# The first three loads of a kernel's middle stage, moved by one step and behind another load

## The chip, the cores and the metric

The kernel runs on one core of a Trainium2 chip. A core has a matrix engine (TensorE, PE in the profile; its weight loads are listed apart as PEld), a vector engine (VectorE, DVE), an activation engine (ScalarE, ACT), a general engine (GpSimd, POOL) and a queue engine (SyncE, SP) that here does nothing but issue transfers between memory and the core's on-chip buffers. Each engine works through its own list of instructions in order. Products are accumulated in PSUM banks of 128 x 512 words. The metric is the time of one execution in microseconds; smaller is better.

## The reference

The input `x` has 2048 rows of 576 numbers. Two kinds of layer alternate, each applied to the normalized rows and added to `x`:

```python
x = x + A(layernorm(x), seq_re, seq_im, hid_re, hid_im)
x = x + B(layernorm(x), k, v, shift_k, ssm_k, ssm_D)
x = x + A(layernorm(x), seq_re, seq_im, hid_re, hid_im)
x = x + B(layernorm(x), k, v, shift_k, ssm_k, ssm_D)
```

`A` is the real part of a two-dimensional Fourier transform, written with matrices: `a = x @ hid_re.T`, `b = x @ hid_im.T`, and `y = seq_re @ a - seq_im @ b`. `B` does not need the layer's data until its last step: it forms `kv` from `k`, `v` and a short convolution over four rows, convolves it along the 2048 rows with `ssm_k` (in the reference by an FFT of length 4096), adds `kv * ssm_D`, and multiplies the result into its normalized input. So the long convolution is the same in both `B` layers, and can be computed once, beside the first `A` layer.

## The kernel before

Every product is made in a two-part form: a float32 number is split into a rounded high part (ScalarE, a copy) and a low remainder (VectorE, a subtraction), and three products high-high, high-low and low-high are summed. `split` does it (lines 99 and 100).

**The first layer.** `layer` swaps the order of the two transforms: first along the sequence, then along the hidden axis. It goes through 128 steps, `n` = 0 to 127: four blocks `tb` of 512 output columns, in each the real and the imaginary part (`g`), in each 16 blocks `k` of 128 rows. A step multiplies one row block by one 128 x 512 tile of `c_mat`: twelve products into four banks (named `s`) and two into a fifth (`rm`). `load_c` loads the tile of a step two steps ahead, into a raw buffer of the ring `craw`, and splits it into one of three tiles `cs`. After steps 31, 63 and so on a block is complete; `hidden` multiplies it by the 576 x 576 hidden-axis matrix `W`, in eight half tiles of 27 products each (`bk<-w,u` in the profile), chunk 8 of the reduction last. `added` holds the last addition of such a half tile to the residual (line 289). The eight half tiles of block 0 wait in `pending` and must be done ahead of the last step of block 1's real part, step 47, so that W has to be there then.

**W.** `load_w` is a generator. From step `W_FROM` = 41 on it is called twice a step, in the middle and at the end, until all nine chunks are under way: chunk 8 first, then 0 to 7, so that chunk 6 comes at the end of step 44 and chunk 7 in the middle of step 45. A chunk is 128 x 576 numbers, loaded by SP into one of three buffers `wl` taken in turn, and split into the tile `w`. For the imaginary part (chunks 4 to 7) the sign is turned in the split (ScalarE line 242, VectorE line 243).

**The convolution.** `branch` is a generator that computes `B`'s convolution in three stages beside the first layer: a first Fourier stage (products `bf`, results stored by ScalarE's queue to the tensor `td`), a middle stage of 64 parts that reads `td`, and a last stage. Its F1 stage ends at step 42. The next call of it sets up the middle stage: it lays new rings over buffers of the first stage, cuts the ring `craw` from three raw tiles to two, loads the small matrices `midc` on POOL's queue, and gives out the first three loads from `td` with `load_feed`. These go on SP (line 169), into two tiles in `flts` (ring `land`) and one in the tile `mid`. From step `MID_FROM` = 47 on the middle stage is paced by a cost account: `passed` counts what the layer has done, `spent` what the branch has, and `next(br)` is called while the branch is behind. A part splits its loaded tile (`act_split`: ScalarE line 514, VectorE line 520), multiplies it (three products into each of two banks, `bk<-mid`), forms a complex product (lines 532 to 535), splits, transforms back and stores.

**What sets the order.** The order in which each engine meets its instructions is planned when the kernel is built, by a scheduler that follows the written order where nothing else binds it and the readiness of buffers and data in its own estimate of time. `tc.issue_after(i)` binds it: every instruction written inside that block which goes to `i`'s engine is placed behind `i` on that engine. It adds no wait between engines. `behind(...)` does this for several instructions, and `load_after` puts a load behind the latest load of `c_mat` (`anchor[-1]`).

**Around the change.** In the loop over the first layer, at line 808, stands the call that sets up the middle stage:

```python
        if whole is not None and not part and n >= W_FROM and len(W) < 9:
            with behind(*stored):
                next(wl)
        if whole and n == MID_LOAD:
            next(br)
```

`whole` is true at the end of a step. The functions that the diff touches:

Of the kernel before, what the change touches and what calls it, by code (L numbers as in the profile page):

```python
# [15 lines left out]
P = 128  # L16
# [19 lines left out]
W_FROM = 41  # L36
HOLD = 125
W_SAVE = 60
MID_LOAD = 44
MID_FROM = 47  # L40
I2_END = 111
PREP = 113
# [24 lines left out]
def fnet_h3_kernel(ctx: ExitStack, tc: tile.TileContext, x, c_mat, w_re, w_im, k_pad, v, shift_k,  # L67
                   ssm_k, ssm_d, f1c, i2c, midc, out):
    nc = tc.nc
# [28 lines left out]
    def split(h, l, src):  # L98
        a = nc.scalar.activation(h, src, AF.Copy).ins  # L99
        return a, nc.vector.tensor_tensor(l, src, h.bitcast(F32), OP.subtract).ins  # L100

    @contextmanager
    def behind(*instructions):
        with ExitStack() as stack:
            for i in instructions:
                stack.enter_context(tc.issue_after(i))
            yield
# [8 lines left out]
    def region_a(dt, name):  # L116
        return sb.tile([P, 9 * 2 * D], dt, tag="ra", name=name)

    def region_b(dt, name):
        return sb.tile([P, 6 * WIDE], dt, tag="rb", name=name)  # L120
# [11 lines left out]
    def lay(t, at, *sizes):  # L132

        for name, words, n in sizes:
            ring.setdefault(name, Ring()).tiles.extend(t[:, at + i * words:at + (i + 1) * words] for i in range(n))
            at += n * words
        assert at <= t.shape[1], (at, t.shape, sizes)
        return at

    def fresh(*names):  # L140
        for name in names:
            ring[name] = Ring()

    def two(v):
        return v.rearrange("p (a n) -> p a n", a=2)
# [16 lines left out]

    anchor, made, rounded, pows, biased, halved, added, evac, parted, stored = [], [], [], [], [], [], [], [], [], []

    scaled = []

    def load_after(dst, src):
        with tc.issue_after(anchor[-1]):
            return nc.sync.dma_start(dst, src).ins
# [57 lines left out]
    def load_w():  # L227
        lay(flts, SC_AT + CRAW * NT + 4 * D, ("wl", D, 3))
        wg = region_a(FR, "w").rearrange("p (k n) -> p k n", k=9)
        for ch in (8, *range(8)):  # L230
            w = two(wg[:, ch])
            raw = ring["wl"]()
            if ch < 8:
                nc.sync.dma_start(raw, (w_re if ch < 4 else w_im)[(ch % 4) * P:(ch % 4 + 1) * P, :])
            else:
                nc.sync.dma_start(raw[:REM], w_re[NC * P:, :])
                nc.sync.dma_start(raw[REM:], w_im[NC * P:, :])
            for lo, hi, sg in ((0, P, 1 if ch < 4 else -1),) if ch < 8 else ((0, REM, 1), (REM, P, -1)):
                if sg > 0:
                    split(w[lo:hi, 0, :], w[lo:hi, 1, :], raw[lo:hi])  # L240
                else:
                    nc.scalar.activation(w[lo:hi, 0, :], raw[lo:hi], AF.Copy, scale=-1.0)
                    nc.vector.scalar_tensor_tensor(w[lo:hi, 1, :], raw[lo:hi], -1.0,  # L243
                                                   w[lo:hi, 0, :].bitcast(F32), op0=OP.mult,
                                                   op1=OP.subtract)
            W[ch] = w
            yield
        for ch in range(9):
            load_after(w_d[ch], wg[:, ch].bitcast(F32))
            yield  # L250
# [42 lines left out]
    def finish(pending, pieces):  # L293
        while pending and pieces:
            if not isinstance(pending[0], types.GeneratorType):
                pending[0] = hidden(*pending[0])
            if next(pending[0], 0) == 0:
                pending.pop(0)
            else:
                pieces -= 1  # L300
# [433 lines left out]
    def advance(j=None):  # L734
        while to_store:
            load_after(*to_store.pop(0))
        with behind(*halved, *added, *evac):
            for row in list(making):
                if next(row, 0) == 0:
                    making.remove(row)  # L740
            if j is not None:
                making.append(make_x1(j))
                next(making[-1])
# [22 lines left out]
    lay(flts, SC_AT, ("craw", NT, CRAW))  # L766
    br = branch()
    wl = load_w()
    load_x(0)
    warm()  # L770
# [21 lines left out]
    for n, whole in layer(get_x0, lambda j: x[:, j, :], done0, pending):  # L792
        part = whole == "part"
        if part:
            whole = False
        if (whole or whole is not None and n % J < J - 1) and n <= F1_END and not part:
            at = n if whole else n - 0.5
            at16 = 4 + 2 * F1_16
            want = int(4 + F1_16 * at / 8 if at <= 16 else at16 + (68 - at16) * (at - 16) / (F1_END - 16))
            with behind(made[min(n + 2, J - 1)], *evac):  # L800
                while used < want:
                    next(br)
                    used += 1
        if whole is not None and not part and n >= W_FROM and len(W) < 9:
            with behind(*stored):
                next(wl)
        if whole and n == MID_LOAD:
            next(br)
        if n >= MID_FROM:
            if whole is not None:  # L810
                share = (5 if whole else 3) if n % J < J - 1 else (8 if whole else 6)
                passed += STEP * share / 14 * BORDER.get(n % J, 1.05)
            if whole is None or whole and n % 2 == 1 and n % (2 * J) < J - 1 and pending:
                finish(pending, 1)
                passed += PIECE
            while spent < work * min(1.0, passed / total):
                with behind(*added, *evac):
                    spent += next(br, work)
        if not whole:
            continue  # L820
        if n >= W_SAVE and n % 2 == 0:
            next(wl, 0)
        m = n - PREP
        if m == 0:
            lay(flts, SC_AT + CRAW * NT + 2 * D, ("xa", D, 2), ("yb", D, 2))
            old = ring["craw"]
            held = [old(), old()]
            fresh("craw")
            lay(flts, SC_AT + CRAW * NT + 6 * D, ("craw", NT, 1))
            ring["craw"].tiles.extend(held)  # L830
            gate = region_b(F32, "gate")
            lay(gate, 0, ("xa", D, 4), ("yb", D, 4), ("xj", D, 2))
        if 0 <= m and n < HOLD:
            advance(m // 2 if m % 2 == 0 and m < 2 * EARLY else None)
# [340 lines left out]
```

## Time and profile before

| | |
|---|---|
| median of 3 runs | 1185.11 us (1184.79 to 1185.26) |
| the profiled execution, its own time | 1183.61 us |
| its span (first to last instruction) | 1181.8 us |
| TensorE busy | 1167.8 us, 99% |
| VectorE, ScalarE busy | 868.6 us, 650.8 us |
| granted TensorE clock, mean | 0.999 |

In rows of instructions the columns are: start in microseconds, duration, engine, line of the kernel, operation, what is written and read, shape, the count of instructions merged in the row, and in brackets how long the engine had stood idle before it and what released it. Names such as `s`, `bk`, `mid`, `w` are tiles of the program. `SPq` and `ACTq` are the parts of SP and ScalarE that issue transfers; their rows show the issue, not the transfer itself. The steps of the layer are counted here by the pairs of `rm` products: the pair at 206.85 us is that of step 46.

### The profile page before, as it was taken

The numbers are of one execution on the slowest core, as the hardware profiler recorded it, in microseconds if no ns is written. First come the engines' busy times: TensorE is split into PE (matmuls) and PEld (weight loads), VectorE is DVE, ScalarE is ACT, GpSimd is POOL, SyncE is SP. The second block draws the span as 40 slices with busy tenths as digits, with TensorE's granted clock in tenths as the row PEclk, the third lists the DMA queues.
The fourth block names the chain that finished last, engine by engine and source line by source line (L and its number), as shares of the span: only waits on it lengthen the run. The fifth ranks groups of instructions, "written<-read, shape, count | busy, mean of one in ns | idle before, by whom it ended". The sixth has DMA issues, their size and how long they took to land.

```text
span 1181.8 us, 18082 instructions
## 1 busy us (share of the span) xinstructions
PE 1167.8 (99%) x6198; PEld 989.1 (84%) x6198; DVE 868.6 (73%) x1564; ACT 650.8 (55%) x1280; POOL 75.5 (6%) x115
## 2 busy tenths in 40 slices
PE   8999999999999999999999999999999999999997
PEld 6776667988888888888888898888888888889997
DVE  7899983788877778787756765865776777774764
ACT  8865655577766667766645666534444445550210
POOL 2310000000000000001101111000000000001111
PEclk9999999999999999999999999999999999999999
DMA  9879898546666656648966777762872787894621
GB/s 336 284 232 316 263 300 272 160 152 173 213 214 193 203 168 193 190 140 247 270 192 215 249 240 231 247 253 73 257 249 72 221 284 258 260 338 144 219 93 40
DMA packets 147453, 255.64 MB, mean 216 GB/s; under 512 B 16161, under 2 KB 56353, under 8 KB 147362
## 3 DMA queue, kind: packets, MB, share of 16 engines
q1 hardware_dynamic: 111890, 210.17, 55.6%
q10 hardware_dynamic: 28560, 37.91, 9.2%
q0 software_dynamic: 6912, 6.43, 2.5%
q8 instruction: 48, 0.79, 0.3%
q14 instruction: 43, 0.35, 0.1%
HBM read 187.80 MB, written 66.65 MB: 215 GB/s over the span
## 4 chain that ended last, share of the span: by engine, by line
PE 77%; ACT 2%; DVE 2%; DMA 1%; issue 1%; ACTq 0%; DVEq 0%
PE s L76 43%; PE bk L76 30%; PE rm L76 4%; ACT flts L514 1%; ACT mid L514 1%; DVE mid L520 0%; DMA flts<-td 0%; DMA flts<-in_c_mat 0%; ACT mats L99 0%; DVE flts L534 0%; DVE flts L533 0%; DVE flts L532 0%; DVE flts L535 0%; ACTq L550 0%; ACT u L99 0%
## 5 line engine op out<-in xcount | busy, mean ns | idle before, releaser
L76 PE MATMUL s<-mats 128*128 128x512 f32 x2102 | 545.9, 395 | 4.2 <-ACT mats L197 2.4
L76 PEld LDWEIGHTS s<-mats 128*128 128x128 f32 x2102 | 382.7, 188 | 86.1 <-issue 10.9
L100 DVE TENSOR_TENSOR mats<-flts,mats 128x512 fp32r<-128x512 f32 x206 | 140.6, 686 | 50.3 <-ACT mats L99 48.9
L99 ACT ACTIVATE mats<-flts 128x512 fp32r<-128x512 f32 x206 | 128.2, 627 | 81.8 <-PE bk L76 30.7
L76 PE MATMUL bk<-mid 128*128 128x288 f32 x704 | 126.7, 300 | 2.1 <-DVE flts L289 0.8
L76 PEld LDWEIGHTS bk<-mid 128*128 128x128 f32 x704 | 108.6, 188 | 23.0 <-ACT flts L514 5.9
L514 ACT ACTIVATE flts<-bk 128x288 f32<-128x288 f32 (+1 forms) x192 | 76.5, 405 | 90.4 <-PE bk L76 71.6
L76 PE MATMUL bk<-w,u 128*128 128x288 f32 x864 | 120.6, 295 | 0.4 <-DVE w L243 0.4
L76 PEld LDWEIGHTS bk<-w,u 128*128 128x128 f32 x864 | 117.4, 188 | 3.5 <-ACT flts L514 0.9
L520 DVE TENSOR_TENSOR mid<-flts,mid 128x576 fp32r<-128x576 f32 (+1 forms) x149 | 93.3, 627 | 19.1 <-ACT mid L514 16.4
L76 PE MATMUL rm<-mats 128*128 128x512 f32 x304 | 94.5, 390 | 0.2 <-ACT flts L514 0.2
L514 ACT ACTIVATE mid<-flts 128x576 fp32r<-128x576 f32 (+1 forms) x148 | 80.5, 576 | 10.3 <-DVE flts L535 5.1
L289 DVE TENSOR_TENSOR flts<-flts,bk 128x288 f32<-128x288 f32 x48 | 21.8, 453 | 68.3 <-PE bk L76 65.9
L76 PE MATMUL bk<-mats 128*128 128x288 f32 (+1 forms) x376 | 67.8, 317 | 0.0
L76 PEld LDWEIGHTS rm<-mats 128*128 128x128 f32 x304 | 56.9, 188 | 12.6 <-ACT flts L514 0.6
L453 ACT ACTIVATE flts<-bf 128x384 f32<-128x384 f32 (+1 forms) x104 | 43.2, 462 | 43.4 <-PE bf L76 43.2
L76 PE MATMUL s<-t,mats 128*128 128x512 f32 x264 | 64.9, 389 | 0.0
L186 POOL TENSOR_TENSOR flts<-flts 128x1 f32<-128x1 f32 x34 | 28.0, 823 | 515.6 <-DVE flts L185 513.2
L76 PE MATMUL bk<-mats,t 128*128 128x288 f32 (+1 forms) x368 | 59.3, 303 | 0.0
L514 ACT ACTIVATE flts<-flts 64x288 f32<-64x288 f32 x128 | 56.6, 443 | 4.5
L76 PEld LDWEIGHTS bk<-mats 128*128 128x128 f32 x376 | 55.6, 188 | 3.4
L76 PEld LDWEIGHTS s<-t,mats 128*128 128x128 f32 x264 | 49.6, 188 | 10.3
(152 smaller groups left out, 1495.0 us busy)
## 6 DMA issues: line engine op xcount, KB each, us to landing
flts<-in_c_mat SPq DMA_DIRECT2D x148, 256.0 KB, 3.5
ph<-in_c_mat SPq DMA_DIRECT2D x54, 512.0 KB, 4.0
flts<-in_c_mat SPq DMA_DIRECT2D x30, 512.0 KB, 5.2
flts<-td SPq DMA_DIRECT2D x53, 288.0 KB, 3.1
td<-flts ACTq DMA_DIRECT2D x36, 384.0 KB, 4.2
vd<-flts ACTq DMA_DIRECT2D x64, 144.0 KB, 2.3
flts<-vd SPq DMA_DIRECT2D x32, 288.0 KB, 4.1
ud<-ph ACTq DMA_DIRECT2D x12, 512.0 KB, 6.7
```

Source lines behind the costliest of these rows:

```text
L76: return nc.tensor.matmul(ps, lhsT, rhs, start=first, stop=last, skip_group_check=more).ins
L99: a = nc.scalar.activation(h, src, AF.Copy).ins
L100: return a, nc.vector.tensor_tensor(l, src, h.bitcast(F32), OP.subtract).ins
L186: pows.append(nc.gpsimd.tensor_tensor(rs, ve, mhalf, OP.pow).ins)
L289: added[:] = [nc.vector.tensor_tensor(r[:, cs], r[:, cs], ps[:, :HD], OP.add).ins]
L453: stored[:] = [nc.scalar.activation(so[:, i, :], ps[i], AF.Copy).ins]
L514: last_act.append(nc.scalar.activation(*args, **kw).ins)
L520: nc.vector.tensor_tensor(l, src, h.bitcast(F32), OP.subtract)
```

## The change

`MID_LOAD` goes from 44 to 45, so that the middle stage is set up at the end of step 45 and no longer of step 44. `load_w` keeps the instruction of its latest load in a list `asked`, and the call stands in `behind(*asked)`. At the end of step 45 that is the load of chunk 7. What the call gives to SP, the three loads from `td`, is thereby placed behind it on SP's list. The load of `midc` on POOL is not bound by this, since the bound instruction is SP's, but it is written a step later too. The start of the paced work (`MID_FROM`) stays.

```diff
-MID_LOAD = 44
+MID_LOAD = 45
...
-    scaled = []
+    scaled, asked = [], []
...
             if ch < 8:
-                nc.sync.dma_start(raw, (w_re if ch < 4 else w_im)[(ch % 4) * P:(ch % 4 + 1) * P, :])
+                asked[:] = [nc.sync.dma_start(raw, (w_re if ch < 4 else w_im)[(ch % 4) * P:(ch % 4 + 1) * P, :]).ins]
...
         if whole and n == MID_LOAD:
-            next(br)
+            with behind(*asked):
+                next(br)
```

## The prediction

> **What bounds the kernel now.** The page's head and first part come first, then busy time by stretch (start and end, length, then busy time and instructions of PE, PEld, DVE, ACT and POOL, then the granted clock, the share of the DMA engines and GB/s).
>
> ```profile
> span 1181.8 us, 18082 instructions
> ...
> PE 1167.8 (99%) x6198; PEld 989.1 (84%) x6198; DVE 868.6 (73%) x1564; ACT 650.8 (55%) x1280; POOL 75.5 (6%) x115
> ```
>
> ```profile
> 200.00:207.00 7.00, 7.00 (x32) 5.79 (x32) 1.08 (x2) 1.94 (x3) 0.00 (x0) 1.00 0.98 327
> 207.00:215.00 8.00, 6.85 (x45) 5.87 (x44) 5.32 (x8) 3.93 (x8) 0.00 (x0) 1.00 0.52 153
> 215.00:1160.00 945.00, 943.33 (x5061) 821.66 (x5061) 682.99 (x1258) 511.65 (x1001) 48.78 (x77) 1.00 0.65 206
> ```
>
> TensorE is busy 1167.8 of 1181.8 us. The change is made at step 45 of the first layer, near 200 us, so it can reach only idle time behind that: 8.00 - 6.85 = 1.15 us between 207 and 215, and 945.00 - 943.33 = 1.67 us over the 945 us that follow. The granted clock is 1.00 in these stretches, so no time hides in it. What can be won is 1.15 us at the place itself and 2.8 us at the very most; what can be lost has no such limit. The eight microseconds at 207 decide, so I read each engine's own order there, TensorE first.
>
> ```profile
> 206.85 0.62 PE L76 MATMUL rm<-mats 128*128 128x512 f32 x2
> 207.31 3.06 PE L76 MATMUL bk<-w,u 128*128 128x288 f32 x22
> 210.75 0.92 PE L76 MATMUL bk<-w,u 128*128 128x288 f32 x5 [0.38 <-DVE w L243]
> 211.51 0.43 PE L76 MATMUL bk<-mid 128*128 128x288 f32 x2
> 211.77 0.62 PE L76 MATMUL s<-mats 128*128 128x512 f32 x2
> 213.16 0.40 PE L76 MATMUL bk<-mid 128*128 128x288 f32 x1 [0.76 <-DVE flts L289]
> ```
>
> The two `rm` products end step 46. Then the first half tile of `hidden` runs, 27 products with W's nine chunks in order, three to a chunk. It halts after 22, that is inside the eighth chunk in the order 0 to 8: chunk 7, the one loaded last. Its low part, written by VectorE in line 243, is late by 0.38 us. The first products of the middle stage (`bk<-mid`) follow, and the third of them waits 0.76 us for a bank that the add of line 289 frees. The two waits make 1.14 of the 1.15 us. ScalarE and VectorE show where they come from.
>
> ```profile
> 204.03 0.69 ACT L242 ACTIVATE w<-flts 128x576 fp32r<-128x576 f32 x1 [4.69 <-DMA flts<-in_w_im]
> 205.75 0.69 ACT L516 ACTIVATE mid<-flts 128x576 fp32r<-128x576 f32 x1 [1.03 <-DMA flts<-td]
> ...
> 207.15 0.63 ACT L99 ACTIVATE mats<-flts 128x512 fp32r<-128x512 f32 x1
> 207.83 0.69 ACT L514 ACTIVATE mid<-flts 128x576 fp32r<-128x576 f32 x1
> ...
> 209.21 0.69 ACT L242 ACTIVATE w<-flts 128x576 fp32r<-128x576 f32 x1
> 211.26 0.63 ACT L99 ACTIVATE mats<-flts 128x512 fp32r<-128x512 f32 x1 [1.36 <-DMA flts<-in_c_mat]
> ```
>
> ```profile
> 207.82 0.69 DVE L100 TENSOR_TENSOR mats<-flts,mats 128x512 fp32r<-128x512 f32 x1
> ...
> 209.93 0.76 DVE L243 SCALAR_TENSOR_TENSOR w<-flts,w 128x576 fp32r<-128x576 f32 x1
> 211.93 0.69 DVE L100 TENSOR_TENSOR mats<-flts,mats 128x512 fp32r<-128x512 f32 x1 [1.24 <-ACT mats L99]
> 212.65 0.46 DVE L289 TENSOR_TENSOR flts<-flts,bk 128x288 f32<-128x288 f32 x1
> 213.02 1.42 DVE L520 TENSOR_TENSOR mid<-flts,mid 128x576 fp32r<-128x576 f32 x2
> ```
>
> ScalarE splits chunk 5 at 204.03, then waits 1.03 us for the first middle load, and splits both middle loads (205.75, 207.83) ahead of chunk 7 (209.21). The second wait is a longer chain: a c_mat load is late, ScalarE loses 1.36 us before 211.26, VectorE's half of that split starts only at 211.93, and the add of line 289 stands behind it, though its 27 products had ended at 210.75 + 0.92 = 211.67.
>
> **The change part by part.** SP's queue in this stretch, with its waits between 195 and 203 us:
>
> ```profile
> 198.80 0.33 SPq L169 DMA_DIRECT2D mid<-td  x1
> 199.24 0.37 SPq L234 DMA_DIRECT2D flts<-in_w_im  x1
> 199.66 0.47 SPq L281 DMA_DIRECT2D flts<-in_x  x1
> 201.18 0.33 SPq L169 DMA_DIRECT2D flts<-td  x1
> 201.60 0.58 SPq L234 DMA_DIRECT2D flts<-in_w_im  x1
> 202.23 0.43 SPq L169 DMA_DIRECT2D flts<-in_c_mat  x1
> 202.70 1.47 SPq L169 DMA_DIRECT2D flts<-td  x1
> 204.22 0.43 SPq L169 DMA_DIRECT2D flts<-in_c_mat  x1
> 204.69 0.43 SPq L234 DMA_DIRECT2D flts<-in_w_im  x1
> ```
>
> ```profile
> 208.54 4.44 SPq L169 DMA_DIRECT2D flts<-in_c_mat  x3
> ```
>
> ```profile
> SPq L169 <- DMA td<-flts: 3.9, 2, 2.9
> SPq L281 <- DMA td<-flts: 1.4, 1, 1.4
> ```
>
> ```profile
> 196.98 0.76 DVE L100 TENSOR_TENSOR w<-flts,w 128x576 fp32r<-128x576 f32 x1 [3.85 <-ACT w L99]
> ...
> 198.98 0.75 DVE L243 SCALAR_TENSOR_TENSOR w<-flts,w 128x576 fp32r<-128x576 f32 x1
> 199.64 0.68 DVE L100 TENSOR_TENSOR mats<-flts,mats 128x512 fp32r<-128x512 f32 x1
> ```
>
> ```profile
> 195.80 0.53 POOL L173 DMA_DIRECT2D mid<-in_midc  x1 [42.56 <-PE bf L76]
> ```
>
> ```profile
> flts<-in_w_im SPq DMA_DIRECT2D x3, 288.0 KB, 4.8
> ```
>
> Moved are three 288 KB loads from `td`, the one load of `midc` on POOL's queue (its first user is the product at 211.51), and the point at which the c_mat ring goes from three tiles to two. No byte, product or split is added or removed.
>
> First, *the queue.* The three `td` loads (198.80, 201.18, 202.70) stand today among chunks 5, 6 and 7 (199.24, 201.60, 204.69). Two of them waited for the stores to `td`, 3.9 us together, and held what was behind them. Chunk 5's buffer (three in turn, last held by chunk 2) is free at 196.98 + 0.76 = 197.74, its load is issued at 199.24: 1.5 us lost. Chunk 7's buffer, last held by chunk 4, is free at 198.98 + 0.75 = 199.73 and its load goes at 204.69: 5.0 us lost. With the `td` loads behind it I put chunk 5 at 197.8; chunk 6 behind the residual load, which keeps its own wait for a store, at about 200.1; the next c_mat load at 200.5; and chunk 7 at about 201.1. With the 4.8 us to landing of the W rows, chunk 7 is there at 205.9 and VectorE's half done by 205.9 + 0.69 + 0.76, some 207.4. TensorE reaches its low part at 210.75 - 0.38 = 210.37. The 0.38 us go, with 3 us in hand; even if chunk 7 gained only the half of that it would be in time.
>
> On what the shuffle can win, the share of the DMA engines bears: 0.98 at 327 GB/s between 200 and 207, so chunk 7 gains what the `td` loads lose. The Trainium skill, "Trainium Kernel Development and Optimization", section Key Constraints, says that DMAs of the SP, ACT and POOL queues all run on the same 16 engines and interleave. By that rule the last of these loads would land no sooner than today and only their order would change, a sum no different from mine; the 0.98 agrees.
>
> Second, *what is late next: the middle loads.* They now go behind chunk 7, at 201.6 or later, against 198.80 to 202.70 today. The one issued at 201.18 released ScalarE at 205.75, 4.57 us later. By that the first lands at about 206.2, and its split, 0.69 us, ends at 206.9, against 206.44 today. The first product that reads it starts at 211.51, or 211.13 without the 0.38. So a load issued by 211.13 - 0.69 - 4.57 = 205.9 costs nothing, and mine has 4 us to spare. VectorE's halves (line 520) are held behind the add of line 289 by `behind(*added, ...)`, in both kernels. `midc` on POOL waits for the last product that reads the tile's old content (`PE bf`, released at 195.80). One step is 14 products, at 0.62 us for two at most 4.3 us: issued by 200.1, and with the 4.57 us of a load of like size there at 204.7, 6 us ahead of its first product. I cost it at nothing; without that cover each microsecond past 211.13 would cost one.
>
> Third, *the c_mat ring.* When the first part of the middle stage starts, the ring drops its third tile. A step later means that the load for step 47 still takes the third tile, and each of the loads for 48 and 49 takes the tile that was used one load earlier than today. The load for 49 is the first of the three at 208.54, and it waited for the split of 47 that ended at 207.82 + 0.69 = 208.51. Now it waits for the split of 46, over at 199.64 + 0.68 = 200.32. It goes with the load for 48, near 205, and ScalarE's 1.36 us before 211.26 go. VectorE then has nothing in front of the add when the 27 products end at 211.67 - 0.38 = 211.29, and frees the bank at 211.8. TensorE gets there at 211.13 plus two products of the middle and two of step 47 (213.16 - 0.76 - 211.51 = 0.89 us) = 212.0. So the 0.76 us go also. Next comes line 520, two halves in 1.42 us: 211.29 + 0.46 + 0.71 = 212.5 at the earliest for the first. TensorE has one product of the middle (0.40 us) to do from 212.0, so if nothing of step 47 stands between, as it does at 211.77, it waits about 0.1 us there.
>
> The sum: -0.38 - 0.76 + 0.1 = -1.0 us. Bounds: -1.15 and 0 for the two waits themselves. The profiled execution took 1183.61 us, 1.5 us under the median of 1185.11; its time would become 1182.6 and the median 1184.1, which is my forecast, 0.09% below. A measurement of this kernel tells about 0.2% (2.4 us) from no change, so this counts as the same.
>
> **The rivals.**
> - *The wait moves.* ScalarE and VectorE work in their written order, and the new order may put a middle split that waits for its load ahead of something TensorE needs, as today at 205.75 (1.03 us). Then TensorE stands 1.1 us at 211 for another reason: 1185.1. For it speaks that the `td` loads lose what chunk 7 wins; against it the 4 us to spare.
> - *The middle loads come too late* (slower). The new order on SP is planned afresh, and a `td` load may fall behind the c_mat loads that wait for VectorE (three issues from 208.54 to 212.98). The place is the product at 211.51, the point from which it costs is an issue at 205.9. Behind the first of the three, at 208.9, TensorE stands 3.0 us in place of 1.14, +1.9; behind all three, at 213.0, 7.1 us, +6.0. The middle, +4.0, gives 1189.1. More than 2.4 us over today needs an issue after 205.9 + 1.14 + 2.4 = 209.4. For it: a product waiting there holds the whole in-order queue. Against it: the loads for 48 to 50 are written behind the three `td` loads, and 48 is issued at 204.22.
> - *More than the place is won* (faster). The shifted c_mat tiles and an earlier start would also remove the 1.67 us that TensorE loses after 215. All of it gone gives 1185.11 - 1.15 - 1.67 = 1182.3, which is just over 0.2%. Against it: the loads in those 945 us go on as before, and the order there is set by the same costs.
>
> **How the numbers follow.** The forecast has 0.50, with a range of its own from 1183.6 to 1185.0; the moved wait 0.17; the late middle loads 0.23; the wider gain 0.10. The first two lie within 0.2%: same 0.67, slower 0.23, faster 0.10. The range goes from 1182.3, all idle time gone, to 1189.1, the middle of the late loads; half of that rival lies above it, 0.12, and little else outside.
>
> **What would show it.** Right: SP shows chunk 7's load before the three `td` loads and near 201; the row of five `bk<-w,u` products with 0.38 from `DVE w L243` is gone; ScalarE has no 1.36 us for in_c_mat near 211; the add of line 289 starts within 0.3 us of its products; TensorE is busy over 7.8 of the 8 us from 207. Wrong: a TensorE wait for `ACT mid` or `DVE mid L520` near 211, a `td` load issued after 205.9, or idle time that grows in the stretch from 215 to 1160.

## The result and the profile after

The changed kernel takes 1182.28 us (median of 15 runs), the kernel before 1183.75 us in the 15 runs beside it. The ratio is 0.9983, with a 95% interval from 0.9976 to 0.9990. Two later comparisons gave 0.9977 (0.9967 to 0.9987) and 0.9982 (0.9973 to 0.9991). The medians lie 1.47 us apart and the means of the same runs, 1182.02 and 1183.98 us, 1.96 us; the ratio agrees with the means. So the change makes the kernel 0.2% faster, about 2 us, where 1.0 us was forecast. The time lies 0.02 us under the range that was given, 1182.3 to 1189.1. In the two later comparisons the changed kernel took 1183.00 and 1182.49 us, which is inside it.

The order of the instructions as built differs between the two kernels only around steps 44 to 49, on SP, ScalarE and VectorE. TensorE's list and POOL's are the same throughout. This makes the two traces easy to lay side by side. First busy time by stretch after the change, in the columns used in the prediction:

```profile
207.00:215.00 8.00, 8.00 (x54) 7.35 (x53) 4.72 (x9) 4.13 (x8) 0.00 (x0) 1.00 0.63 195
215.00:1160.00 945.00, 942.99 (x5061) 821.66 (x5060) 682.48 (x1257) 511.13 (x999) 48.78 (x77) 1.00 0.65 205
```

All 1.15 us of idle time at the place are gone. Behind 215 us nothing was won: 2.01 us idle against 1.67. TensorE's rows at the place, after the change:

```profile
207.90 3.71 PE L76 MATMUL bk<-w,u 128*128 128x288 f32 x27
211.45 0.44 PE L76 MATMUL bk<-mid 128*128 128x288 f32 x2
211.72 0.63 PE L76 MATMUL s<-mats 128*128 128x512 f32 x2
212.25 0.37 PE L76 MATMUL bk<-mid 128*128 128x288 f32 x1
212.46 0.63 PE L76 MATMUL s<-mats 128*128 128x512 f32 x2
...
213.95 2.31 PE L76 MATMUL bk<-w,u 128*128 128x288 f32 x16
```

The 27 products run through, and the third product of the middle stage follows without a wait. From the first product of the first half tile to the first of the second, which I call the stretch, 213.95 - 207.90 = 6.05 us pass. In the trace before that was 7.64 us: the first product at 207.31 stands in the prediction, and the second half tile began at 214.95, as this row of the trace before shows:

```profile
214.95 3.77 PE L76 MATMUL bk<-w,u 128*128 128x288 f32 x27
```

The stretch is 1.59 us shorter, though the idle time shown was 1.15. Where SP, ScalarE and VectorE stand after the change:

```profile
191.77 0.33 SPq L169 DMA_DIRECT2D flts<-in_c_mat  x1
193.75 0.33 SPq L234 DMA_DIRECT2D flts<-in_w_im  x1
196.65 2.41 SPq L281 DMA_DIRECT2D flts<-in_x  x2
199.50 1.40 SPq L234 DMA_DIRECT2D flts<-in_w_im  x3
200.96 0.85 SPq L169 DMA_DIRECT2D flts<-in_c_mat  x1
203.67 0.81 SPq L169 DMA_DIRECT2D flts<-td  x2
204.58 0.38 SPq L169 DMA_DIRECT2D flts<-in_c_mat  x1
205.19 0.32 SPq L169 DMA_DIRECT2D mid<-td  x1
```

```profile
205.59 1.24 ACT L242 ACTIVATE w<-flts 128x576 fp32r<-128x576 f32 x2
207.76 0.63 ACT L99 ACTIVATE mats<-flts 128x512 fp32r<-128x512 f32 x1 [0.92 <-DMA flts<-in_c_mat]
208.51 0.69 ACT L516 ACTIVATE mid<-flts 128x576 fp32r<-128x576 f32 x1
```

```profile
206.48 1.42 DVE L243 SCALAR_TENSOR_TENSOR w<-flts,w 128x576 fp32r<-128x576 f32 x2
...
210.58 0.69 DVE L100 TENSOR_TENSOR mats<-flts,mats 128x512 fp32r<-128x512 f32 x1 [1.47 <-ACT mats L99]
211.65 0.45 DVE L289 TENSOR_TENSOR flts<-flts,bk 128x288 f32<-128x288 f32 x1 [0.38 <-PE bk L76]
```

Chunks 5, 6 and 7 are issued in one run from 199.50 to 200.90; chunk 7, the last of them, goes at 200.47, where it went at 204.69. Both its halves are done by 206.48 + 1.42 = 207.90, some 2.9 us ahead of use, since ScalarE now splits it ahead of the middle loads too. The load for step 47 now goes at 191.77, into the third tile of the ring, where it went at 202.23. The load for step 49 goes at 204.58 in place of 208.54. The add of line 289 waits for nothing but its products.

### The profile page after: what moved, and what is told of

It reads as the page before. It is cut to its first block, busy times and chain, and to the rows that moved or that the text cites. A ratio compares the mean times of both kernels' runs of the same rounds, so it can differ in the third digit from the quotient of the medians.

```text
span 1180.9 us, 18086 instructions
## 1 busy us (share of the span) xinstructions
PE 1168.1 (99%) x6198; PEld 990.1 (84%) x6198; DVE 868.5 (74%) x1564; ACT 650.9 (55%) x1280; POOL 75.5 (6%) x115
## 4 chain that ended last, share of the span: by engine, by line
PE 86%; DVE 5%; ACT 3%; DMA 3%; issue 2%; SPq 0%; ACTq 0%; POOL 0%; DVEq 0%
PE s L76 49%; PE bk L76 30%; PE rm L76 5%; PE bf L76 2%; DMA flts<-in_c_mat 1%; ACT flts L514 1%; DVE f1f L395 1%; DVE f1f L400 1%; DVE mats L100 1%; ACT mid L514 1%; DVE mid L520 1%; DMA early<-in_x 0%; ACT mats L99 0%; DMA yb<-flts 0%; DMA flts<-td 0%
```

## The experiments

All kernels below have the same order on TensorE at the place, so the stretch can be read in each, from the rows of the two `bk<-w,u` starts. The ratio is to the kernel before, from timed runs.

| kernel | stretch, us | ratio (95% interval) |
|---|---|---|
| before, first profile | 7.64 | |
| changed, three profiles | 6.05, 6.06, 6.06 | 0.9983, 0.9977, 0.9982 |
| step alone, not bound | 6.06 | 0.9981 (0.9973 to 0.9990) |
| ring alone | 6.57 | 0.9985 (0.9976 to 0.9994) |
| loads alone | 6.85 | 0.9988 (0.9979 to 0.9997) |
| step 46 | 6.05 | 0.9979 (0.9970 to 0.9989) |
| bound behind chunk 6, step 44 | 7.68 | 0.9993 (0.9984 to 1.0002) |
| chunk 7 loaded twice | 6.08 | 0.9980 (0.9971 to 0.9989) |
| first middle load made twice | 6.55 | 0.9979 (0.9970 to 0.9988) |
| before, repeated | 8.64 | 1.0000 (0.9992 to 1.0009) |
| before, four more profiles, no timed runs | 8.44, 8.22, 7.77, 8.69 | |

**The step alone.** The binding to chunk 7's load is left out.

```diff
-            with behind(*asked):
-                next(br)
+            next(br)
```

> MID_LOAD = 45 without the binding to chunk 7's load. On SP the middle loads then stand among W's chunks again, but the c_mat ring keeps its third tile for step 47 as in the change. Measure in the trace: from the first product of the first half tile of hidden to the first product of the second (before 214.95 - 207.31 = 7.64 us, after 213.95 - 207.90 = 6.05 us). Theory (two separate waits: chunk 7 late, and a c_mat load late through the ring): the bank wait goes by the ring, chunk 7's wait stays at least in part, 6.7 to 7.0 us, -0.6 to -0.9 us of the whole. Rival (the order of the loads alone makes both): 7.6 us, no gain.

The stretch took 6.06 us, the whole gain: neither theory had it so. SP in this kernel:

```profile
197.24 0.33 SPq L169 DMA_DIRECT2D mid<-td  x1
197.67 0.44 SPq L234 DMA_DIRECT2D flts<-in_w_im  x1
...
201.30 0.33 SPq L169 DMA_DIRECT2D flts<-td  x1
201.68 0.90 SPq L234 DMA_DIRECT2D flts<-in_w_im  x2
202.62 0.42 SPq L169 DMA_DIRECT2D flts<-td  x1
```

Two middle loads still stand ahead of chunk 7, but it is issued near 202.2 and comes in time. With the step moved, the binding has no further effect that these runs can show.

**The ring alone.** In the kernel before, the lines that drop the third c_mat tile become a function `trim`, called at step 45; the middle loads stay at step 44, unbound.

```diff
         if whole and n == MID_LOAD:
             next(br)
+        if whole and n == 45:
+            trim()
```

> The kernel before, with the three middle loads given out at step 44 and not bound; only the dropping of the third c_mat tile is moved behind step 45. Theory: as for the step alone, the wait for the bank (0.85 us between starts) goes and chunk 7's (0.62 us) stays: 6.7 to 7.0 us for the stretch. Rival (the order of the loads alone makes both): 7.6 us.

```profile
207.42 3.06 PE L76 MATMUL bk<-w,u 128*128 128x288 f32 x22
210.69 0.93 PE L76 MATMUL bk<-w,u 128*128 128x288 f32 x5 [0.22 <-DVE w L243]
...
213.99 2.30 PE L76 MATMUL bk<-w,u 128*128 128x288 f32 x16
```

The wait for the bank is gone, a part of the wait for chunk 7 stays. The stretch of 6.57 us is a little under the 6.7 that was expected, and the ring is shown to be a cause of its own.

**The loads alone.** The changed kernel with `trim()` called at step 44, ahead of the load for step 47.

```diff
+        if whole and n == 44:
+            trim()
         if whole and n == MID_LOAD:
             with behind(*asked):
                 next(br)
```

> The changed kernel, with the third c_mat tile dropped at step 44 as before, so that the load for step 49 waits for the split of 47 again. Theory: chunk 7's wait is gone, and the bank wait is back as far as the load for 49 is late: 6.5 to 6.9 us for the stretch. Rival (the order of the loads alone makes both): 6.05 us, the whole gain.

```profile
207.00 3.71 PE L76 MATMUL bk<-w,u 128*128 128x288 f32 x27
...
212.15 0.37 PE L76 MATMUL bk<-mid 128*128 128x288 f32 x1 [0.69 <-DVE flts L289]
...
213.85 2.31 PE L76 MATMUL bk<-w,u 128*128 128x288 f32 x16
```

```profile
207.27 0.68 ACT L242 ACTIVATE w<-flts 128x576 fp32r<-128x576 f32 x1 [1.13 <-DMA flts<-in_w_im]
...
210.16 0.63 ACT L99 ACTIVATE mats<-flts 128x512 fp32r<-128x512 f32 x1
```

The wait for chunk 7 is gone and the wait for the bank is there, as expected. Its way is not quite the one I had in mind. ScalarE does not wait for the c_mat load here; it comes to that split late, because it waited 1.13 us for chunk 7. The load for step 47, which the third tile lets go at 191.77, now goes among W's chunks (200.18). So the ring seems to help in two ways: the load for 49 waits for an earlier split, and one load less competes with W's last chunks. No run here parts the two.

**One step more.** `MID_LOAD = 46`, with the binding.

> MID_LOAD = 46 with the binding: the middle stage is set up one step later still. Theory: chunk 7 and the ring stay as well served as in the change, and the middle loads, issued near 204 to 206, land in time: 6.05 us for the stretch, the same gain. Rival (late middle loads): each microsecond of issue past 205.9 us costs one, 7 us or more for the stretch.

The stretch takes 6.05 us, the same gain. But the middle loads did not go near 204 to 206, as was expected:

```profile
202.19 0.81 SPq L169 DMA_DIRECT2D flts<-td  x2
```

```profile
207.12 3.71 PE L76 MATMUL bk<-w,u 128*128 128x288 f32 x27
```

They go 207.12 - 202.19 = 4.9 us ahead of the first half tile, against 207.90 - 203.67 = 4.2 us in the change. So one step more does no harm, and this run did not test late middle loads.

**Behind chunk 6.** `MID_LOAD = 44` with the binding, which then takes chunk 6's load.

> MID_LOAD = 44 with the binding: the middle loads stand behind chunk 6's load, not chunk 7's, and the third c_mat tile is dropped at step 44. Theory: chunks 5 and 6 come earlier, chunk 7 comes early enough for its slack of some 2 us and its wait goes (0.62 us), the late c_mat load of step 49 comes back with the ring (up to 0.85 us): 6.1 to 6.9 us. Rival (only a place behind chunk 7 helps): 7.6 us.

```profile
207.55 3.71 PE L76 MATMUL bk<-w,u 128*128 128x288 f32 x27
...
213.52 0.37 PE L76 MATMUL bk<-mid 128*128 128x288 f32 x1 [1.51 <-DVE flts L289]
...
215.23 0.98 PE L76 MATMUL bk<-w,u 128*128 128x288 f32 x6
```

```profile
211.53 0.63 ACT L99 ACTIVATE mats<-flts 128x512 fp32r<-128x512 f32 x1 [0.66 <-DMA flts<-in_c_mat]
```

My expectation failed. The wait for chunk 7 went, but the wait for the bank grew from 0.76 to 1.51 us: with two c_mat tiles, ScalarE reached the split of 49 only at 211.53. That is 3.98 us after the first product of the half tile, and in the kernel before it was 211.26 - 207.31 = 3.95. So the bank comes free as late as before; TensorE, no longer held by chunk 7, only gets there sooner and waits longer. The end is that of the rival "the wait moves", but not by its mechanism: what holds ScalarE is the c_mat load, not a middle split. The stretch is 7.68 us, the ratio's interval holds 1, so that with the c_mat load as late as before, taking away chunk 7's wait won nothing that the timed runs can tell.

**Chunk 7 twice.** In the changed kernel chunk 7's load is followed by a second, equal one.

```diff
+                for _ in range(1 if ch == 7 else 0):
+                    nc.sync.dma_start(raw, w_im[(ch % 4) * P:(ch % 4 + 1) * P, :])
```

> The changed kernel, with chunk 7 loaded a second time into the same buffer behind the first load, so that chunk 7 comes some 4 to 5 us later. It probes what a wait of TensorE costs. Theory: the 23rd product waits, and the stretch grows by the idle time that the profile shows plus some 0.25 us, since the busy time ahead of a halt takes in the drain of the last product; in the change the slack was 210.8 - 207.9 = 2.9 us, so some 1.5 to 2 us of idle time shown. Rival (idle time shown is the whole cost): the growth equals the idle time.

The second load, and chunk 7's split on ScalarE and VectorE:

```profile
205.06 0.33 SPq L236 DMA_DIRECT2D flts<-in_w_im  x1
```

```profile
208.21 0.69 ACT L244 ACTIVATE w<-flts 128x576 fp32r<-128x576 f32 x1 [0.18 <-DMA flts<-in_w_im]
```

```profile
208.92 0.76 DVE L245 SCALAR_TENSOR_TENSOR w<-flts,w 128x576 fp32r<-128x576 f32 x1 [1.81 <-ACT w L244]
```

It landed 3.15 us after its issue, not the 4 to 5 that I had expected, and the low part was ready at 209.68, just ahead of the 23rd product, due at 206.93 + 22 x 0.13, some 209.8. No wait came, so this run says nothing on what a wait costs. It does show the room that the change gives: chunk 7 was ready 2.75 us after the first of the 27 products (206.93) and not 0.0 us after it, and the stretch took 6.08 us in place of 6.06.

**The first middle load twice.** In the changed kernel the first of the three `td` loads is made twice into its buffer.

```diff
+                for _ in range(1 if i == 0 else 0):
+                    load_after(landed[i], t_d[4 * q:4 * q + 4, :, hf * D:(hf + 1) * D].rearrange("m j d -> (m j) d"))
```

> The changed kernel, with the first middle load made twice into the same buffer, so that it comes some 4.5 us later, as if it were issued near 208.5 us. It probes the forecast's slower rival. Theory: it lands near 213, its split ends near 213.8, and the first product of the middle stage, due at 211.45, waits some 2 to 2.5 us for it: the stretch takes 8 to 8.6 us. Rival (other work fills the gap, or the load isn't needed yet): 6.1 us.

The second load on SP, its split, and the first product that reads it:

```profile
207.90 0.32 SPq L169 DMA_DIRECT2D flts<-td  x1
```

```profile
210.96 0.68 ACT L516 ACTIVATE mid<-flts 128x576 fp32r<-128x576 f32 x1 [0.93 <-DMA flts<-td]
```

```profile
211.69 0.53 PE L76 MATMUL bk<-mid 128*128 128x288 f32 x2 [0.39 <-ACT mid L516]
```

This is the mechanism of the slower rival, and it exists: TensorE waits for the middle load, and the stretch grows by 6.55 - 6.06 = 0.49 us, far from the 8 to 8.6 us that were expected. The timed runs (0.9979) do not show so small a loss. But the load landed in 3.06 us and not in the 4.57 of the crowded queue, so the point from which it costs lies about 1.5 us later than the 205.9 that I had worked out: 207.90 - 0.49 = 207.4.

**The kernel before, again.** The kernel before, timed against itself, with the changed kernel beside both; the changed kernel was also timed beside the last three kernels.

> The kernel before, unchanged, put in the place of a changed one, to see what the comparison gives where nothing differs, and for a second profile of it. Theory (the gain is the 1.6 us of the stretch, and what the ratios show beyond it is scatter of the comparison): the ratio is 0.9993 to 1.0, as for the kernel bound behind chunk 6, whose stretch gained nothing; the stretch is 7.6 us again. Rival (the change gains some 0.7 us outside the stretch): the ratio is 1.0000 within 0.0003.

> The changed kernel in the same rounds as the repeated kernel before. Theory: its ratio lies 0.0013 to 0.0014 (1.6 of 1184 us) below that of the repeated kernel before; the stretch takes 6.06 us. Rival (gain outside the stretch): 0.002 or more below it.

> The changed kernel once more, for its time beside those of the next kernels and a second profile. Theory (all of the gain is made between 207 and 215 us): the stretch from the first product of the first half tile to the first of the second takes 6.0 to 6.1 us, the whole is 1.6 us below the kernel before. Rival (part of it lies elsewhere): the whole differs from before by more than the stretch does, 2 us or more.

The ratio of the kernel before to itself is 1.0000 (0.9992 to 1.0009), so the comparison has no offset that it can show, and the changed kernel in these rounds is at 0.9982, between what theory and rival expected. The gain is larger than the 1.59 us of the first two traces. But the stretch in this second profile of the kernel before is 8.64 us, where 7.6 was expected:

```profile
207.48 2.92 PE L76 MATMUL bk<-w,u 128*128 128x288 f32 x21
211.12 0.40 PE L76 MATMUL bk<-w,u 128*128 128x288 f32 x1 [0.71 <-ACT w L242]
211.91 0.93 PE L76 MATMUL bk<-w,u 128*128 128x288 f32 x5 [0.39 <-DVE w L243]
...
214.32 0.40 PE L76 MATMUL bk<-mid 128*128 128x288 f32 x1 [0.75 <-DVE flts L289]
...
216.12 2.05 PE L76 MATMUL bk<-w,u 128*128 128x288 f32 x14
```

Here TensorE waits for chunk 7 twice, first for its high part and then for its low part. On SP the first middle load, which waits for a store to `td`, goes a microsecond later than in the first profile (198.80), and chunk 5 behind it:

```profile
199.86 0.33 SPq L169 DMA_DIRECT2D mid<-td  x1
200.30 0.38 SPq L234 DMA_DIRECT2D flts<-in_w_im  x1
```

Whether 7.64 us or 8.64 us is the rule was left open by this, so four more profiles of the kernel before were taken.

> The kernel before, a third profile. The first two show a stretch (first product of the first half tile to first product of the second) of 7.64 and 8.64 us, the changed kernel 6.05, 6.06 and 6.06. Theory (chunk 7's landing scatters with the traffic, and the change took the scatter away with the wait): 7.6 to 8.7 us, differing from profile to profile. Rival (7.64 is the rule and 8.64 an outlier): 7.6 to 7.7 us.

> The kernel before, a fourth profile: as for the third, theory 7.6 to 8.7 us for the stretch with the excess in the wait for chunk 7 and not in the wait for the bank; rival 7.6 to 7.7 us.

> The kernel before, a fifth profile: theory 7.6 to 8.7 us for the stretch; with five or six of them the mean less 6.06 us should be the 2 us that the timed runs show (ratio 0.9977 to 0.9983). Rival: 7.6 to 7.7 us, mean 1.6 us above the changed kernel.

> The kernel before, a sixth profile, as for the fifth: theory 7.6 to 8.7 us for the stretch, rival 7.6 to 7.7 us.

They show 8.44, 8.22, 7.77 and 8.69 us. The first profile was the shortest of six. Their mean is 8.23 us, which is 2.17 us above the 6.06 of the changed kernel: 2.17 / 1184 = 0.18%, a ratio of 0.9982. That is what the timed runs gave. Against the same mean the single stretches of three other kernels also give ratios close to the measured ones: ring alone 0.9986 (measured 0.9985), loads alone 0.9988 (0.9988), behind chunk 6 0.9995 (0.9993). The first middle load made twice fits least, 0.9986 against 0.9979. The intervals are some 0.001, or 1 us, to each side, so a few tenths of a microsecond elsewhere would not be seen.

In five of the six profiles both waits are there; in the fifth (7.77) only chunk 7's. What scatters most is chunk 7: ScalarE's split of it starts 1.90, 2.90, 2.73, 2.46, 2.90 and 2.91 us after the first product of the half tile, in the order of the profiles. In the fifth the first middle load went at 198.96, almost as early as in the first, and yet chunk 7 is late; ScalarE waited there for the next middle load, which was issued at 202.62:

```profile
208.80 0.69 ACT L514 ACTIVATE mid<-flts 128x576 fp32r<-128x576 f32 x1 [0.92 <-DMA flts<-td]
...
210.17 0.68 ACT L242 ACTIVATE w<-flts 128x576 fp32r<-128x576 f32 x1
```

So a late store to `td` is not all of it; landing times scatter as well, and what sets them is not shown.

## Why the prediction was wrong

The direction was right and the mechanism in the main, and the size of the terms was not.

- *The terms.* The step that failed is the sum "-0.38 - 0.76 + 0.1 = -1.0 us" and the bound "-1.15 and 0 for the two waits themselves". The two waits, with what hangs on them, cost 2.17 us in the mean of six profiles. Two things made them too small. First, they were taken from one profile, and a wait for a transfer has its own scatter: the stretch ran from 7.64 to 8.69 us, and the profile at hand was the low end. Second, idle time as shown is less than the cost of a halt. In that same profile the stretch lost 1.59 us against 1.14 us shown. From the trace before, the 22nd and 23rd products started 0.68 us apart, where the usual distance is 0.13, so this halt of "0.38" cost 0.55; at the bank, the distance of 1.16 against 0.29 after the change makes 0.87 of "0.76". By the rows, the stretch lost 4.20 - 3.55 = 0.65 us up to the first product of the middle stage, 1.65 - 0.80 = 0.85 from there to the third, and 1.79 - 1.70 = 0.09 from there to the second half tile, 1.59 in all. The +0.1 for line 520 did not come: products of step 47 stood between, and no wait is shown there.
- *The upper bound of the gain.* Of "1.15 us at the place itself and 2.8 us at the very most" the first falls with it, as a bound from one execution's idle time. The second was not passed, but only because it counts 1.67 us behind 215 that stayed.
- *Two waits as two separate terms.* The sum adds them. The kernel bound behind chunk 6 shows that they hang together: there chunk 7's wait was gone and the c_mat load as late as before, and the wait for the bank grew by 0.75 us.
- *The range.* It began at 1182.3, worked out from the median of 1185.11 of three runs. Beside the changed kernel the kernel before had a median of 1183.75, and the forecast did not allow the base itself to move. With that base even the too small gain of 1.0 would have given 1182.75. So it is partly chance that the time fell outside, by 0.02 us, and the size of the gain is what the forecast had wrong: 1.0 us against about 2. The forecast also held that a measurement could not tell less than 2.4 us from no change; it told these 2 us.
- *The queue.* Right: chunk 7 went 4.2 us earlier and its low part was ready at 207.90, where 207.4 was forecast; the trace after runs 0.6 us behind the other at step 46. Wrong in a detail: chunk 5 did not go at 197.8 but at 199.50, since both residual loads (`in_x`) now stand ahead of it and wait for stores, 4.2 us together.
- *The middle loads.* Their slack was put at 4 us; they were issued at 203.67 and not 201.6, held by the wait for a store to `td`. They were still in time, and the rival of late middle loads did not come. Brought about in a kernel of its own it costs what its mechanism says, from a later point.
- *The c_mat ring.* Right that it is a cause of its own and removes the wait for the bank: the ring alone does so. It seems to do more than forecast, as the load for step 47 leaves the crowd around W.
- *The binding*, which gave the change its words, is not needed: the later step alone gives the whole 6.06 us.
- *The wider gain* past 215 us did not come: 2.01 us idle against 1.67.

## What to carry to other kernels

A wait that ends in a transfer is a sample. Before it is priced, look at it in several profiles, or put a range around it from the landing times that the queue shows. And price a halt of a pipelined engine by the distance between starts with and without it, not by the idle time shown. When a call is moved, list everything that happens inside it: here the moved call also shrank a ring of buffers, and that alone gave 1.66 of the 2.17 us. The loads alone gave 1.38; the two overlap, so neither can be priced as what is left when the other is taken off.

## What the runs showed that I had not expected

The changed kernel's stretch is the same to 0.01 us in three profiles, while the kernel before scatters by 1.05 us in six. At this place the change removed a source of scatter as well as the waits: in these three profiles TensorE waits there for nothing. The whole time still scatters from elsewhere, 1181.19 to 1183.35 us in the same three executions. And a load of 288 KB that took 4.57 us to land, with the share of the DMA engines at 0.98 meanwhile, took 3.15 and 3.06 us when issued a few microseconds later, at shares of 0.85 and 0.78. In the fifth profile of the kernel before one took 208.80 - 202.62 = 6.18 us.
